# Rewriting the hand-made order of the first quarter in a fused attention and feed-forward kernel

## The chip, the cores and the metric

The kernel runs on one core of one Trainium2 chip. The metric is the device time of one execution in microseconds (us). The engines are named PE (TensorE), DVE (VectorE), ACT (ScalarE), POOL (GpSimd) and SP (SyncE, which here only issues DMAs).

## The reference

Two layers follow each other. The first is attention in which a query sees only the keys of its own cluster: 4 batches, 8 heads, 768 positions, head width 64, 16 clusters per head. The second is a feed-forward layer on the 3072 tokens of width 512, with a softmax-weighted activation of width 1024 and a layer norm.

```python
q_assign = np.argmax(np.einsum('bhsd,hcd->bhsc', q_n, c_n), axis=-1)
k_assign = np.argmax(np.einsum('bhsd,hcd->bhsc', k_n, c_n), axis=-1)
mask = q_assign[:, :, :, None] == k_assign[:, :, None, :]
scores = np.where(mask, scale * np.matmul(q, k.transpose(0, 1, 3, 2)), -1000000000.0)
attn = softmax(scores); attn_out = np.matmul(attn, v)
...
h = x @ w_in
e = np.exp(h - h_max); solu = h * e / (np.sum(e) + 1e-09)
ln = (solu - mu) / np.sqrt(var + 1e-06) * g_ln
return ln @ w_out
```

## The kernel before

The work is cut into 1,814 named steps. Each step has an engine, and each engine works through its steps in one fixed order, which stands as text in the table ORDER (L28 to L72): "xa2 ca E6" is two steps of kind xa, one of kind ca, six of kind E, each time the next of that kind on that engine. A second table, AWAY (L73 to L90), names steps that run on another engine than their default. No step is reordered when the kernel runs: an engine waits at the head of its queue.

One pair of heads (b.p, batch and pair) goes through these steps. SP loads q and k (ld, L375, L433) and v (lv, L551). For batch 0, PE transposes q and k into PSUM (tp, L385) and ACT or DVE evacuates them into a tile xt (xa and xb, L411); for later batches DVE transposes from SBUF instead (xt, L441). A cast (ca, L460) copies a head's 64 rows to bf16 in the tile qk; an index of 1 in the third place means k, which is scaled as it is cast (L472), and 0 means q (L470). PE multiplies xt by the cluster centres (cl, L475). DVE transposes that back (tb), takes the maximum of each group of 16 (mx), compares (oh) and transposes the one-hot rows (ot, L494 to L521). Four placements (pl, L525) copy the one-hot rows beneath q and k in qk, so that one matmul gives scores plus a cluster bias, and bl (L547) zeroes the rows of the odd head. cv (L557) casts v, one step a head.

S is a bank of scores (PE, L618), E its exponential (ACT, L632), V the product with v (PE, L645), and N divides by the row sum (DVE, L658). S22.0 is the first score bank of unit 22. Batch 0 has units 0 to 21: 0 to 3 are pair 0, and the others come two to a group; S4.0 begins pair 1, S8.0 pair 2, S12.0 pair 3, S16.0 turns back to the last columns of all three, and S22.0 begins batch 1. There is one PSUM region for the products V, so the first V of a group waits for the N of the group before it (V2.0 for N0, V4.0 for N1, V8.0 for N3, and so on).

Scores of units 4 to 17 also use two of the three banks of hreg. After that hreg belongs to the feed-forward layer: for a tile f of 128 tokens, tx turns x, h (PE, L742) multiplies by w_in, hm (DVE, L748) takes the maximum, ex (ACT, L753) the exponential, u (DVE, L759) the product, tu turns it, bn and ag (DVE) give the variance, at and al (POOL, L781 and L787) the scale, y (PE, L798) multiplies by w_out, sc scales and ou writes. Once, near the start, w_out is loaded in four parts (lo), summed with its gains on DVE (su0 to su7, L593), averaged by PE (me) and centred by DVE (ce0 to ce7, L606) while the mean stands in a bank of hreg; h1.0.0 needs ce7. w_in is loaded in four parts (li) and cast in eight (wi, POOL). at0 needs ex0.

cp, cb, cq and cf prepare the centres, gt and gk the gains, z and sg are memsets, and fl and wm are matmuls on a blank tile. po is a name in POOL's order with no instruction behind it.

Of the kernel before, what the change touches and what calls it, by code (L numbers as in the profile page):

```python
# [22 lines left out]
class Weave:  # L23
# [19 lines left out]
        fl wm tp2 cp fl4 cl tp2 fl4 cl fl tp S2 cq S tp S tp S2 tp S tp2 S2 cl S V3 S2 tp3 S gt V3
        S2 tp2 S tp S2 cl S3 V3 S7 V3 S3 cl S3 V4 S5 V2 S V2 S4 V S2 V3 S cl S3 V2 S V S2 V S me S3
        V S V3 me S3 ptx V2 S2 cl V S V S5 V2 h4 S2 h V2 S3 h V2 S V2 S h S2 h S V S V2 S V S h S2 h
        V S2 V2 S y3 V S2 y S h2 S2 V2 h2 S2 cl S V S V2 S V S h S2 h S V S V S h y4 S3 V3 h2 S2 V2
        S h S2 V y S y3 S2 V2 S cl S V S V S V2 S2 y S y S2 V3 S2 y S V S y S2 V2 S h S2 V3 S2 cl S
        V3 S3 cl S2 V2 S V2 S h2 S3 h V S V S V2 y3 S2 y V S2 V h S2 V S h S V S h2 S3 h V2 S2 V4 h
        S3 y3 S2 V y S2 V3 S2 h2 S3 V2 cl S3 V2 h S2 h cl V2 S2 V2 S h S2 h2 S2 V3 y S y S y S y V S
        V2 S h2 S2 h2 S3 V3 S V y3 V y V S2 h S cl S3 V2 h S2 h V S2 V S cl V2 S3 y2 S V S V y2 h2  # L50
        S2 V2 S h2 S3 cl S V3 S V S2 y3 S2 V y V S h S2 h V2 S h2 S3 h V2 S y2 S V2 S2 V2 y2 S2 h3
# [5 lines left out]
        cn xb cb tb mx oh ot pl2 tb mx oh ot xa3 cf ca bl cv tb mx oh ot ca2 xa gk su2 N tb mx xa oh
        cv ot su N su2 tb mx N oh su ot N xt2 N su tb mx su oh N xt2 N ce tx ce3 N ce4 hm N ot u N
        bn hm tb N mx oh bn ag ot u xt2 hm cv N bn u bn2 tb mx hm bn N oh ag2 u ot xt2 hm bn N sc u
        bn tb ag cv N xt mx oh xt ot sc N bl xt2 tb bn N mx ca tb N mx oh ot hm oh N ot u xt bn3 ag  # L60
        xt N ag hm sc N ca u bn2 xt bl sc hm ag N xt tb mx u tb oh ot N hm mx xt oh u bn2 ot N hm bn
# [1263 lines left out]
```

## Time and profile before

| what | value |
|---|---|
| median of 3 runs | 223.92 us (223.9 to 224.23) |
| profiled execution, first to last instruction | 222.4 us |
| PE busy | 214.8 us, 97% |
| DVE busy | 199.1 us, 90% |
| ACT busy | 194.7 us, 88% |
| POOL busy | 126.6 us, 57% |
| HBM read and written | 23.11 MB and 6.29 MB |

The profile is of one execution, and its span leaves out what lies before the first and behind the last instruction, so it is 1.5 us under the runs' median. A busy PE is not a PE at its peak, since matmuls are pipelined and their ends are modelled. The same holds for ACT and DVE rows: one instruction's duration overlaps the next one's, so the cost of one in a full queue is the distance between starts. A wait is put down to the semaphore that came last by the profile; where the engine named had long been done, another was the cause.

### The profile page before, as it was taken

To read this page: it belongs to the slowest core of one execution; us is meant where nothing else is said; L and a number is where in the kernel's file an instruction comes from. 1 tells how busy PE (TensorE), PEld (TensorE's weight loads), DVE (VectorE), ACT (ScalarE), POOL (GpSimd) and SP (SyncE) were. 2 spreads that over 40 slices of the span, in tenths; PEclk is the share of its full clock that TensorE was granted. 3 is DMA by queue.
4 is the path that set the end of the run, shared out by engine and by line. 5 is a ranking of instruction groups with operands and counts; after the bars stand their busy time and mean duration, and the time that the engine had idled before them with its cause. 6 is when DMAs were issued, how large, how long until landed. Compare 5 with 4: busy or idle time off the path is not lost.

```text
span 222.4 us, 6852 instructions
## 1 busy us (share of the span) xinstructions
PE 214.8 (97%) x2518; PEld 151.8 (68%) x2548; DVE 199.1 (90%) x363; ACT 194.7 (88%) x382; POOL 126.6 (57%) x252
## 2 busy tenths in 40 slices
...
GB/s 157 352 388 221 193 165 284 203 172 165 127 175 237 180 141 215 136 193 166 153 211 239 156 185 150 151 168 158 230 99 50 115 78 145 117 165 121 166 98 143
DMA packets 122433, 38.74 MB, mean 174 GB/s; under 512 B 111448, under 2 KB 117152, under 8 KB 122400
## 3 DMA queue, kind: packets, MB, share of 16 engines
...
q10 hardware_dynamic: 720, 0.49, 0.7%
...
q14 instruction: 13, 0.11, 0.1%
HBM read 23.11 MB, written 6.29 MB: 132 GB/s over the span
## 4 chain that ended last, share of the span: by engine, by line
PE 91%; DVE 3%; issue 2%; ACT 2%; DVEq 0%; ACTq 0%
PE sps L627 27%; PE hreg L744 18%; PE yps L813 17%; PE ops L654 16%; PE csc L489 4%; PE hreg L627 2%; PE idle_p L859 2%; PE csc L484 1%; PE hreg L403 1%; PE hreg L396 1%; ACT qk L468 1%; PE hreg L813 1%; ACT e L635 1%; DVE u L763 1%; DVE w_sum L598 1%
## 5 line engine op out<-in xcount | busy, mean ns | idle before, releaser
L635 ACT ACTIVATE e<-sps 128x512 bf16<-128x512 f32 (+1 forms) x276 | 143.2, 609 | 10.2 <-PE sps L627 9.8
L627 PE MATMUL sps<-qk 96*128 96x256 bf16 (+5 forms) x600 | 87.4, 263 | 0.7 <-ACT e L635 0.4
L627 PEld LDWEIGHTS <-qk 96*128 96x128 bf16 (+1 forms) x636 | 59.6, 121 | 24.5 <-issue 8.8
L654 PEld LDWEIGHTS <-e 128*128 128x128 bf16 x1152 | 49.9, 97 | 9.3 <-issue 1.9
L654 PE MATMUL ops<-v,e 128*128 128x65 bf16 x1152 | 54.3, 193 | 0.4 <-DVE x L679 0.4
L744 PE MATMUL hreg<-w_in_sb,xT 128*128 128x512 bf16 x177 | 48.3, 378 | 0.8
L813 PE MATMUL yps<-w_out_c,uT 128*128 128x512 bf16 x169 | 45.1, 379 | 0.8
L540 POOL COPY qk<-oht 32x384 f32<-32x384 f32 (+1 forms) x49 | 24.2, 494 | 21.5 <-DVE oht L521 15.7
L763 DVE TENSOR_TENSOR u<-e_sb,hreg 128x1024 bf16<-128x1024 bf16 (+1 forms) x25 | 29.1, 1169 | 2.7 <-ACT e_sb L756 2.1
L774 DVE BATCH_NORM_STATS2 bs<-u 128x6 f32<-128x512 bf16 x48 | 31.3, 677 | 0.0
L750 DVE TENSOR_REDUCE nmax<-hreg 128x1 f32<-128x1024 f32 x24 | 29.1, 1213 | 2.0 <-PE hreg L744 1.7
L756 ACT ACTIVATE e_sb<-hreg,nmax 128x1024 bf16<-128x1024 f32 x24 | 26.9, 1121 | 4.5 <-DVE nmax L750 4.4
L790 POOL TENSOR_SCALAR esq<-es,mv 128x1 f32<-128x1 f32 x24 | 8.3, 344 | 33.6 <-DVE mv L778 30.3
L813 PEld LDWEIGHTS <-uT 128*128 128x128 bf16 x200 | 18.0, 97 | 13.1 <-issue 0.3
L744 PEld LDWEIGHTS <-xT 128*128 128x128 bf16 x192 | 17.6, 97 | 11.3 <-ACT e L635 0.3
L472 POOL TENSOR_SCALAR qk<-xt 64x768 bf16<-64x768 f32 (+1 forms) x27 | 22.2, 823 | 3.5 <-DVE xt L444 1.7
L444 DVE STREAM_TRANSPOSE xt<-raw 128x768 f32<-128x768 f32 x24 | 22.2, 949 | 0.0
L470 POOL CAST qk<-xt 64x768 bf16<-64x768 f32 (+1 forms) x25 | 20.9, 836 | 1.2
L679 DVE TENSOR_TENSOR x<-ops,den 128x256 bf16<-128x256 f32 (+1 forms) x39 | 18.9, 486 | 1.3
L784 POOL TENSOR_SCALAR es<-esum 128x1 f32<-128x1 f32 x24 | 5.6, 236 | 20.9 <-ACT e_sb L756 20.4
L793 POOL TENSOR_TENSOR alpha<-esq,halves 128x1 f32<-128x1 f32 x24 | 13.8, 574 | 2.0
L830 ACT ACTIVATE y<-yps,alpha 128x512 f32<-128x512 f32 x15 | 10.4, 695 | 4.3 <-PE yps L813 3.0
...
## 6 DMA issues: line engine op xcount, KB each, us to landing
...
```

The source lines that it names most:

```text
L444: nc.vector.transpose(xt[:], raws[b, p, i][:].rearrange("p j c -> p (j c)"))
L472: VEC[e].tensor_scalar(dst, src, scalar1=inv_C, scalar2=1.0, op0=Alu.mult, op1=Alu.mult)
L540: ins = VEC[e].tensor_copy(dst.bitcast(F32), src.bitcast(F32).unsqueeze(1) .to_broadcast([NB, 2, n // 2]))
L627: ins = nc.tensor.matmul(sps_[n, k][:, c0:c0 + w], side(b, h // 2, 1, h % 2, keys)[r], side(b, h // 2, 0, h % 2, slice(s0 * P, s0 * P + w) ...
L635: ins = nc.scalar.activation(es[n, k][:, :w], sps_[n, k][:, :w], Act.Exp, scale=exp_scale, bias=-exp_scale)
L654: nc.tensor.matmul(opss[g][:, s, :VW], es[n, k][:, c0:c0 + P], v1[slot(b, h // 2)][:, h % 2, kt, :VW], start=(kt == 0), stop=(kt == n_t - 1))
L744: uses(nc.tensor.matmul(hreg[:, at(f, f2)[1], :], xTs[f][:, dc, :], w_in_sb[:, dc, f2 * FF2:(f2 + 1) * FF2], start=(dc == 0), stop=(dc == ...
L750: uses(nc.vector.tensor_reduce(ff[f, "nmax"][:], pair_of(f), axis=AXY, op=Alu.max, negate=True), *both(f))
L756: uses(nc.scalar.activation(ff[f, "e"][:], pair_of(f), Act.Exp, bias=ff[f, "nmax"][:], accum_out=ff[f, "esum"][:]), *both(f))
L763: uses(nc.vector.tensor_tensor(ff[f, "u"][:, r], ff[f, "e"][:, r], pair_of(f)[:, r], op=Alu.mult), *both(f)[r])
L774: nc.vector.bn_stats(ff[f, "bs"][:, f2, :], ff[f, "u"][:, f2, :])
L813: ins = nc.tensor.matmul(dst, ff[f, "uT"][:, at(f, f2)[0] * (n_fc // 2) + c, :], w_out_c[:, fc, cols], start=(fc == fcs[0] and turn == 0 i ...
```

## The change

The two tables are written anew up to about the first fourth of the run, and nothing else is. The steps, their work and their needs are the same. Each engine's order is new up to these points, and the same behind them: PE up to y0.0, DVE up to u2, ACT up to E3.0, POOL up to at1 (and the name po moves from its end to its start), SP up to the loads of batch 1's third pair.

These steps change engine:

| step | from | to |
|---|---|---|
| xa0.1.0.0, xa0.1.1.0, xa0.3.0.1, xa0.3.1.1 | DVE | ACT |
| xa0.1.1.1, xa0.2.0.0 | ACT | DVE |
| ca0.0.1.0.1 (half a head of k) | ACT | POOL |
| ca0.0.1.1.1 (half a head of k) | POOL | DVE |
| ca0.2.1.0 (k) | ACT | DVE |
| ca0.1.1.0, ca0.1.1.1, ca0.3.1.1 (k) | POOL | DVE |
| ca0.1.0.0, ca0.1.0.1 (q), ca0.2.1.1 (k) | DVE | POOL |
| cv0.0.0, cv0.1.0 | DVE | POOL |
| cv1.1.1 | POOL | DVE |
| pl0.0.1.1.1, pl0.0.1.0.0 (half a pair) | POOL | DVE |

```diff
     ORDER["DVE"] = """
-        cn xb cb tb mx oh ot pl2 tb mx oh ot xa3 cf ca bl cv tb mx oh ot ca2 xa gk su2 N tb mx xa oh
-        cv ot su N su2 tb mx N oh su ot N xt2 N su tb mx su oh N xt2 N ce tx ce3 N ce4 hm N ot u N
...
+        cn xb cb tb mx oh ot pl2 tb mx xa oh ot cf pl xa bl pl ca xa ca tb mx ca oh gk ot su N ca su
+        xt tb mx oh ot su2 N su tb mx oh N ot su xt ca N su tb su N xt mx oh ot N ce2 N ce tx xt N
...
     ORDER["ACT"] = """
-        wa xa2 ca2 xa2 xb ca4 E6 xa E2 xa E xa ca E3 xa3 E4 ca E2 xa E53 ex E13 ex E5 sc E3 ex E11
+        wa xa2 ca2 xa2 xb ca3 xa E2 xa E6 xa E xa ca E3 xa2 E3 xa E2 xa E xa E53 ex E13 ex E5 sc E3
...
     ORDER["SP"] = """
-        ld4 si ld3 lv lg ld3 lo lv lo ld2 lo2 lv ld6 lv ld8 li4 tx ld3 lv ld tx lv tu ld10 tx tu ld4
+        ld4 si ld3 lv lg ld3 lo lv ld4 lo2 ld lv li ld3 lo ld4 lv ld li ld3 li2 tx ld lv tx ld4 lv
...
```

Three places show the new order best. The line numbers of the new kernel are two higher. The first is DVE from the end of pair 3's cluster search (mx, oh, oht are its maximum, one-hot rows and turned rows) to N3; den and x are the two instructions of an N, w_sum is an su, xt<-raw is a transpose of batch 1, and qk_102<-xt is a cast for pair 3. Before:

```order
L510 TENSOR_REDUCE mx<-cst 128x24
L666 RECIPROCAL den<-ops 128x4
L679 TENSOR_TENSOR x<-ops,den 128x2x2x64
L515 TENSOR_TENSOR oh<-cst,mx 128x384
L598 SCALAR_TENSOR_TENSOR w_sum<-w_g,g_ln_115,w_sum 128x512
L521 STREAM_TRANSPOSE oht<-oh 128x384
L666 RECIPROCAL den<-ops 128x4
L679 TENSOR_TENSOR x<-ops,den 128x2x2x64
L444 STREAM_TRANSPOSE xt<-raw 128x768 x2
```

After:

```order
L512 TENSOR_REDUCE mx<-cst 128x24
L517 TENSOR_TENSOR oh<-cst,mx 128x384
L668 RECIPROCAL den<-ops 128x4
L681 TENSOR_TENSOR x<-ops,den 128x2x2x64
L523 STREAM_TRANSPOSE oht<-oh 128x384
L600 SCALAR_TENSOR_TENSOR w_sum<-w_g,g_ln_115,w_sum 128x512
L446 STREAM_TRANSPOSE xt<-raw 128x768
L474 TENSOR_SCALAR qk_102<-xt 64x6x128
L668 RECIPROCAL den<-ops 128x4
L681 TENSOR_TENSOR x<-ops,den 128x2x2x64
```

The last den and x of both pieces are N3. One transpose of batch 1 and a k cast of pair 3 now stand in front of it; the other transpose of batch 1 stands further ahead, in front of pair 2's tb.

The second place is POOL from the blank of pair 1 to that of pair 2. qk_100, qk_101 and qk_102 are the tiles of pairs 1, 2 and 3; qk<-oht is a placement, qk<-xt a cast, v a cast of v. Before:

```order
L549 MEMSET qk_100 16x384
L470 CAST qk_102<-xt 64x6x128
L533 COPY qk_100<-oht 32x6x64
L470 CAST qk_102<-xt 64x6x128
L533 COPY qk_101<-oht 32x6x64
L558 CAST v_1_106<-vf 128x6x64
L1290 MEMSET v_1_106 128x12x2
L1290 MEMSET v_2_107 128x12x2
L533 COPY qk_101<-oht 32x6x64 x3
L472 TENSOR_SCALAR qk_102<-xt 64x6x128
L549 MEMSET qk_101 16x384
```

After:

```order
L551 MEMSET qk_100 16x384
L535 COPY qk_100<-oht 32x6x64 x2
L560 CAST v_1_106<-vf 128x6x64
L472 CAST qk_102<-xt 64x6x128 x2
L535 COPY qk_101<-oht 32x6x64 x2
L560 CAST v_1_106<-vf 128x6x64
L551 MEMSET qk_101 16x384
L535 COPY qk_101<-oht 32x6x64
L560 CAST v_2_107<-vf 128x6x64
L535 COPY qk_101<-oht 32x6x64
```

Pair 2's blank moved ahead of its last two placements, and two casts of v now stand between the placements.

The third place is POOL around at0 (es<-esum). qk_103 is the tile of batch 1's first pair, v_4 its v. Before:

```order
L578 CAST w_in_sb<-w_st 128x512 x7
L470 CAST qk_103<-xt 64x768
L472 TENSOR_SCALAR qk_103<-xt 64x768 x2
L784 TENSOR_SCALAR es_1229<-esum 128x1
L540 COPY qk_103<-oht 32x2x192 x4
L1290 MEMSET v_4_109 128x12x2
L558 CAST v_4_109<-vf 128x6x64
```

After:

```order
L580 CAST w_in_sb<-w_st 128x512 x3
L542 COPY qk_103<-oht 32x2x192 x2
L580 CAST w_in_sb<-w_st 128x512
L542 COPY qk_103<-oht 32x2x192
L580 CAST w_in_sb<-w_st 128x512 x3
L786 TENSOR_SCALAR es_1229<-esum 128x1
L560 CAST v_4_109<-vf 128x6x64 x2
L474 TENSOR_SCALAR qk_103<-xt 64x768
L542 COPY qk_103<-oht 32x2x192
```

Three of the four placements moved ahead of at0, between the casts of w_in; two casts of v and a k cast now stand between at0 and the fourth.

More of the change, by code (lines that the diff above doesn't have):

```diff
@@ L39 @@
-        pl2 al pl2 ca2 bl ca at al ca pl2 cv2 pl ca3 al ca3 pl at2 pl3 al2 ca2 pl ca at cv pl cv at
-        ca at cv al pl2 bl pl al at3 al2 at al2 at al at al2 at2 po at al3
+        po pl2 ca bl z ca pl2 ca2 cv ca cv pl2 ca bl pl2 cv ca2 pl2 cv bl pl cv pl ca pl cv sg pl z
+        pl z bl pl ca cv z wi cv ca wi3 pl2 wi pl wi3 at cv2 ca pl ca3 bl al pl2 ca3 at pl2 z bl ca3
+        al at al pl4 at ca cv ca cv ca cv al bl ca3 pl4 ca2 pl4 at2 pl2 bl ca cv pl al2 ca2 cv2 ca2
+        at cv ca4 al pl4 at2 cv bl cv3 pl2 al pl2 ca2 bl ca at al ca pl2 cv2 pl ca3 al ca3 pl at2
@@ L41 @@
+        pl3 al2 ca2 pl ca at cv pl cv at ca at cv al pl2 bl pl al at3 al2 at al2 at al at al2 at3
+        al3
     """
     ORDER["PE"] = """
[L43 to L51, printed above, removed]
@@ new lines @@
+        me S2 V3 me S2 V S4 V2 S V2 S3 V ptx S V S V2 S2 cl S V S2 h V h3 S V S h V S3 h V2 S V2 S h
+        S2 h S V S V S V2 S h S2 h V S2 V S V y3 V S2 y S h2 S2 V2 h2 S2 cl S V S V2 S V S h S2 h S
+        V S V S h y4 S3 V3 h2 S2 V2 S h S2 V y S y3 S2 V2 S cl S V S V S V2 S2 y S y S2 V3 S2 y S V
+        S y S2 V2 S h S2 V3 S2 cl S V3 S3 cl S2 V2 S V2 S h2 S3 h V S V S V2 y3 S2 y V S2 V h S2 V S
+        h S V S h2 S3 h V2 S2 V4 h S3 y3 S2 V y S2 V3 S2 h2 S3 V2 cl S3 V2 h S2 h cl V2 S2 V2 S h S2
@@ new lines @@
+        h2 S2 V3 y S y S y S y V S V2 S h2 S2 h2 S3 V3 S V y3 V y V S2 h S cl S3 V2 h S2 h V S2 V S
+        cl V2 S3 y2 S V S V y2 h2 S2 V2 S h2 S3 cl S V3 S V S2 y3 S2 V y V S h S2 h V2 S h2 S3 h V2
+        S y2 S V2 S2 V2 y2 S2 h3 S3 V2 h2 V y S3 y3 V3 S3 h2 S2 cl S V S V S V2 S y2 h V S2 h V S2
+        h2 S2 V S V h V4 S2 y2 h S3 V2 h2 S2 V2 S y2 S2 h2 y2 S h2 S2 V2 y S V2 S y h2 S3 h2 S2 V4 y
+        S3 h2 y V S2 h2 V S V S V y4 S2 V h4 S3 y V3 y S2 y2 h4 y S V3 y V y2 h ptx h y h2 y3 h2 y4
@@ L55 @@
+        h2 ptu2 y8 ptu y4 ptu y4
     """
     ORDER["DVE"] = """
[L57 to L61 removed]
```

53 lines of the change are left out of this document (26 added, 27 removed).

## The prediction

> **What bounds the kernel now.** I read the page's span first, then the busy time by stage, then the timeline of each engine at the places where the order changes.
>
> ```profile
> span 222.4 us, 6852 instructions
> 8.00:24.10 16.10, 15.19 (x179) 9.86 (x172) 14.62 (x32) 15.67 (x39) 11.77 (x20) 1.00 0.97 323
> 24.10:34.00 9.90, 9.69 (x148) 7.36 (x149) 9.52 (x19) 9.78 (x22) 8.13 (x15) 1.00 0.87 151
> 34.00:47.10 13.10, 13.05 (x172) 9.31 (x170) 12.56 (x24) 12.93 (x27) 10.14 (x18) 1.00 0.90 242
> 60.00:220.00 160.00, 157.50 (x1754) 109.87 (x1779) 147.50 (x256) 140.33 (x267) 85.30 (x165) 1.00 0.80 157
> ```
>
> Each stage row gives the stretch, its length, the busy time of PE, weight load, DVE, ACT and POOL, the granted clock, and DMA. From 60 us on PE is busy 157.5 of 160 us, with an order that the change leaves alone: a head start there is carried to the end. Before that three engines are full at once. So I ask where PE stands idle in the rewritten stretch, and which engine is late there next. The clock is 1.00 throughout, so no term comes from it.
>
> PE's timeline where the first batch's second head pair begins (start, duration, and idle time in brackets):
>
> ```profile
> 21.42 0.66 PE L627 MATMUL sps<-qk 96*128 96x384 bf16 x3
> 22.46 0.74 PE L654 MATMUL ops<-v,e 128*128 128x65 bf16 x18 [0.38 <-DVE x L679]
> 23.04 0.65 PE L627 MATMUL sps<-qk 96*128 96x384 bf16 x3
> 24.09 0.60 PE L627 MATMUL hreg<-qk 80*128 80x256 bf16 x4 [0.40 <-DVE xt L430]
> 29.58 0.82 PE L627 MATMUL sps<-qk 80*128 80x256 bf16 x6
> 30.24 0.54 PE L654 MATMUL ops<-v,e 128*128 128x65 bf16 x12
> 31.44 1.22 PE L627 MATMUL sps<-qk 96*128 96x256 bf16 x6
> ```
>
> The pace is in the rows from 29.58: six score matmuls of 256 columns go out in 30.24 - 29.58 = 0.66 us, 0.11 each, so three of 384 columns need 0.49. (In the last row six took 1.22: there PE waited for ACT to free score slots.) The first group was out at 21.91 and V2.0 began at 22.46; the second at 23.53 and S4.0 began at 24.09. PE lost 0.55 + 0.56 = 1.1 us, both to DVE: to N0, and to the evacuation xa0.3.1.1 that sat in DVE's queue behind mx0.2. Both go: the new order has N0 right behind su0, and that evacuation on ACT.
>
> **Part 1, ACT.** Four evacuations come to ACT; two evacuations, half a k cast and a full k cast leave.
>
> ```profile
> 8.68 2.02 ACT L468 ACTIVATE qk<-xt 64x384 bf16<-64x384 f32 x4
> 10.61 2.34 ACT L635 ACTIVATE e<-sps 128x384 bf16<-128x384 f32 x6
> 17.19 1.27 ACT L430 COPY xt<-hreg 128x384 f32<-128x384 f32 x3
> 19.83 0.86 ACT L468 ACTIVATE qk<-xt 64x768 bf16<-64x768 f32 x1
> 20.56 0.88 ACT L635 ACTIVATE e<-sps 128x384 bf16<-128x384 f32 x2
> ```
>
> From start to start a half cast takes (10.61 - 8.68) / 4 = 0.48, a full cast 20.56 - 19.83 = 0.73; an evacuation takes 1.27 / 3 = 0.42. ACT loses 0.48 + 0.73 - 2 x 0.42 = 0.4 us net. With that and PE's 1.1 us, S4.0 can come about 1.0 us earlier, at 23.1. What is late next is POOL, whose placements S4.0 needs:
>
> ```profile
> 17.68 2.16 POOL L533 COPY qk<-oht 32x384 f32<-32x384 f32 x3
> 25.23 0.93 POOL L533 COPY qk<-oht 32x384 f32<-32x384 f32 x1 [2.28 <-DMA raw<-in_q_dram]
> 26.92 2.18 POOL L533 COPY qk<-oht 32x384 f32<-32x384 f32 x3
> 30.05 0.41 POOL L549 MEMSET qk<- 16x384 f32 x1
> 45.71 1.72 POOL L472 TENSOR_SCALAR qk<-xt 64x768 bf16<-64x768 f32 x2
> 52.46 0.51 POOL L558 CAST v<-vf 128x384 bf16<-128x384 f32 x1
> L533 POOL COPY qk<-oht x12: 497/614/934, 17.7 to 34.5; 32x384 f32<-32x384 f32 x12
> ```
>
> The first row is pl0.1, and the last gives minimum, median and maximum of a placement in ns. pl0.1 began at 17.68. Now a k cast stands ahead of it on DVE (0.54 to 0.81, below), so it begins at 18.3; four copies, a cast, a blank and 0.4 of gaps (4 x 0.61 + 0.86 + 0.41 + 0.4 = 4.1) end at 22.4, and at 23.7 with all copies at 0.93. I take the median: S4.0 keeps 23.1.
>
> **Part 2, POOL before S8.0.** Before, POOL stood idle 2.28 us until DVE's turned one-hot rows were there (the DMA that the row names had landed), and pl0.2 ended at 26.92 + 2.18 = 29.10, just ahead of S8.0 at 29.58. In the new order a v cast and two q casts follow pl0.1 (22.4 + 0.51 + 2 x 0.86 + 0.2 = 24.8), then come four copies, two v casts and a blank: 4 x 0.61 + 2 x 0.51 + 0.41 and 0.4 of gaps, to 29.1. The head start at S8.0 is then about 0.4, not 1.0; with all copies at 0.93 it would be -0.9. ACT works a few scores behind PE, so I keep its 1.0 us, and let PE catch up where it waited for slots in the row at 31.44.
>
> **Part 3, DVE up to N3.** V8.0 needs N3, the normalisation of the group before it, since there is one output bank group. Four k casts of a full head, half a cast, two placements and two evacuations come to DVE; four evacuations, two q casts, a k cast and two v casts leave; both transposes of batch 1 now stand in front of N3.
>
> ```profile
> 8.99 0.57 DVE L540 COPY qk<-oht 32x192 f32<-32x192 f32 x2
> 11.10 1.45 DVE L430 COPY xt<-hreg 128x384 f32<-128x384 f32 x3
> 14.10 0.36 DVE L558 CAST v<-vf 128x384 bf16<-128x384 f32 x1
> 15.17 0.58 DVE L497 STREAM_TRANSPOSE cst<-csc 128x384 f32<-128x384 f32 x1 [0.71 <-PE csc L484]
> 32.05 1.83 DVE L444 STREAM_TRANSPOSE xt<-raw 128x768 f32<-128x768 f32 x2
> 34.45 0.78 PE csc L489 x8
> L472 DVE TENSOR_SCALAR qk<-xt x3: 541/543/810, 18.1 to 163.9; 64x768 bf16<-64x768 f32 x3
> L470 DVE CAST qk<-xt x4: 541/556/691, 13.1 to 126.8; 64x768 bf16<-64x768 f32 x4
> ```
>
> Coming: 0.57 + 2 x 0.48 + 0.35 + 4 x 0.54 + 1.83 = 5.87. The 0.48 is 1.45 / 3, and the 0.35 an estimate: half of 0.54 to half of 0.81. Leaving: 4 x 0.48 + 0.69 + 0.56 + 0.81 + 2 x 0.36 = 4.70, and the 0.71 of idle time. N3 made way for the transposes at 32.05, so now at 32.05 + 5.87 - 4.70 - 0.71 = 32.5. PE reaches V8.0 from S8.0 at 29.2 by nine score banks of two matmuls, four value products ((23.04 - 22.46) / 3 = 0.19 each) and cl1.0, which is 9 x 0.22 + 4 x 0.19 + 0.78 = 3.5, at 32.7. No wait by this sum; if each k cast takes the 0.81 that one took at 18.1, N3 ends at 33.6 and PE waits 0.9 us.
>
> That 0.81 is the price while POOL was copying: the three copies from 17.68 on took 0.72 each, where the fastest take 0.50. Both engines were slow together. The Trainium skill, Perfetto Trace Analysis, section Optimizing Scalar/DVE Operations, states that GPSIMD and DVE share an SBUF read port, so that moving operations between those two might not help. By that rule the sum would be the 33.6. The two later k casts of 0.54 show that it does not hold each time here.
>
> **Part 4, DVE to the first feed-forward tile.** h1.0.0 needs ce7, ex0 needs hm0.
>
> ```profile
> 34.27 0.18 DVE L666 RECIPROCAL den<-ops 128x4 f32<-128x4 f32 x1 [0.40 <-PE ops L654]
> 44.40 2.71 DVE L607 SCALAR_TENSOR_TENSOR w_out_c<-w_g,g_ln,hreg 128x512 bf16<-128x512 f32 x4
> 47.13 1.23 DVE L750 TENSOR_REDUCE nmax<-hreg 128x1 f32<-128x1024 f32 x1
> 48.86 0.57 DVE L521 STREAM_TRANSPOSE oht<-oh 128x384 bf16<-128x384 bf16 x1
> 48.39 1.11 ACT L756 ACTIVATE e_sb<-hreg,nmax 128x1024 bf16<-128x1024 f32 x1
> ```
>
> From N3 to the end of ce7 (44.40 + 2.71) it was 47.11 - 32.05 = 15.06. The two transposes (1.83) and an idle 0.40 go, ot1.0 (0.57) comes: 13.4. So ce7 ends at 45.9 and hm0 at 47.2 instead of 48.36, 1.2 us earlier; with N3 at 33.6 it is 0.1 earlier. ex0 followed hm0 at once (48.36 to 48.39), so these are the two ends of its head start; ACT's own 1.0 caps the upper. I take 0.65, near the middle, since the copies' median 614 ns against 497 at best says that part of them meet DVE.
>
> **Part 5, POOL before S22.0.** The new order puts two v casts and a k cast between at0 and the last placement of batch 1's first pair; before, four placements followed at0.
>
> ```profile
> 49.75 0.24 POOL L784 TENSOR_SCALAR es<-esum 128x1 f32<-128x1 f32 x1 [2.32 <-ACT e_sb L756]
> 50.05 2.16 POOL L540 COPY qk<-oht 32x384 f32<-32x384 f32 x4
> 52.26 0.38 PE L627 MATMUL sps<-qk 80*128 80x256 bf16 x2
> ```
>
> at0 waits for ex0. From its end at 49.99 the old four took to 52.21, and S22.0 began at 52.26. The new four need 2 x 0.51 + 0.86 + 0.50 and about 0.1 of gaps, 2.48 in place of 2.22. So S22.0 loses 0.25 of the head start: 0.65 - 0.25 = 0.4 us. Nothing behind it in the changed tables waits sooner than before.
>
> The SP order is rewritten too: batch 1's first load goes ahead of the last three quarters of w_out, and DVE turns it well before the 32.05 of the row above. DMA is busy 0.97 in the first stage row, so that load could be late. I take 0, since it also stands further ahead in SP's queue; a late one would cost about what the idle 0.40 at 34.27 did.
>
> **The sum.** The profiled execution's span is 222.4; the runs' median is 223.92, so 1.5 us lie outside the span and stay. 222.4 - 0.4 + 1.5 = 223.5 us. A measurement of this kernel can tell 0.2% (0.45 us) from no change: this forecast lies on that edge.
>
> **Rivals.** *The whole head start comes through:* k casts at 0.54, POOL's copies at 0.50, v casts ready, so ex0 leads by the capped 1.0 and S22.0's placement hides behind PE's own work: 222.9. For it: DVE's later casts; against: the S22.0 sum. *DVE and POOL slow each other (the slower side):* all k casts at 0.81 put N3 at 33.6 and V8.0 waits 0.9 us; hm0 leads 0.1 at best, and lags 0.25 if the placements on POOL and the two sums of su beside them slow down as much; S22.0 takes 0.25 more. It decides from a lead of 0.25 and below at ex0, where nothing is left after S22.0: +0.5, 224.4. For it: 0.81 and 0.72 at 17.7 to 18.9; against: 0.54 later. The page of the Trainium skill named above states the rule behind it. *It changes nothing:* DVE's work cancels its idle time and PE stands where it stood at 52.26: 223.9.
>
> **Chances.** Forecast 0.40 (half of it beyond the edge: 0.19 faster, 0.20 same, 0.01 slower); whole head start 0.22, all faster; slower rival 0.22 (0.18 slower, 0.04 same); nothing 0.16 (0.13 same, 0.02 slower, 0.01 faster). Faster 0.42, same 0.37, slower 0.21. The range 222.8 to 224.5 takes in both outer cases; the forecast's own is 223.2 to 223.8.
>
> **What would show it.** Right: S4.0 near 23.1 and no idle time in front of V2.0 and S4.0; hm0 ending near 47.7; POOL's last placement before S22.0 as PE's releaser. Wrong: PE waiting for N3 at V8.0, DVE k casts at 0.8, hm0 ending after 48.4, xt1.0.0 waiting for its load, or a PE wait at a place that I have not named.

## The result and the profile after

The new order is slower by 0.7%: 225.51 us in the median of four runs (225.4 to 225.77) against 223.95 for the kernel before, a ratio of 1.0071 (95% interval 1.0056 to 1.0086). The forecast was 223.5 us, its range ended at 224.5.

The first view of the changed kernel is its span, then the first two stage rows as shown of before (stretch, length, busy time of PE, weight load, DVE, ACT, POOL, granted clock, DMA), then the waits of PE from 17 to 54 us (total, times, longest).

```profile
span 223.2 us, 6880 instructions
```
```profile
8.00:24.10 16.10, 15.80 (x178) 10.41 (x176) 15.45 (x34) 15.73 (x40) 11.85 (x21) 1.00 0.98 305
24.10:34.00 9.90, 8.40 (x123) 5.62 (x120) 9.51 (x17) 8.83 (x19) 9.14 (x15) 1.00 0.89 215
```
```profile
PE sps L629 <- POOL qk L535: 1.8, 2, 1.5
PE sps L629 <- ACT e L637: 0.2, 1, 0.2
```

In the first stretch PE is busier than before (15.80 against 15.19): the two waits for DVE are gone. In the second it has lost more than it won (8.40 against 9.69 of 9.90 us), ACT with it (8.83 against 9.78), while POOL's busy time rose from 8.13 to 9.14. The clock is 1.00 as before. The waits name the engine, POOL, and the line of the placements. PE's timeline (start, duration, idle time in brackets) shows where:

```profile
22.23 0.96 PE L629 MATMUL sps<-qk 96*128 96x384 bf16 x3
23.03 0.60 PE L629 MATMUL hreg<-qk 80*128 80x256 bf16 x4
...
28.56 0.38 PE L629 MATMUL hreg<-qk 96*128 96x256 bf16 x2
30.44 0.81 PE L629 MATMUL sps<-qk 80*128 80x256 bf16 x6 [1.50 <-POOL qk L535]
...
36.01 0.38 PE L629 MATMUL sps<-qk 80*128 80x256 bf16 x2 [0.34 <-POOL qk L535]
```

The row at 23.03 is S4.0, without a wait, where it stood at 24.09. The row at 30.44 is S8.0, at 29.58 before; the one at 36.01 is S12.0, at 35.40 before. Both now wait for the last placement of their pair. POOL's timeline of the same stretch:

```profile
18.53 1.16 POOL L535 COPY qk<-oht 32x384 f32<-32x384 f32 x2 [1.75 <-DVE oht L523]
19.78 1.67 POOL L474 TENSOR_SCALAR qk<-xt 64x768 bf16<-64x768 f32 x1
21.49 0.41 POOL L551 MEMSET qk<- 16x384 f32 x1
21.94 1.04 POOL L535 COPY qk<-oht 32x384 f32<-32x384 f32 x2
23.04 0.71 POOL L560 CAST v<-vf 128x384 bf16<-128x384 f32 x1
23.70 2.05 POOL L472 CAST qk<-xt 64x768 bf16<-64x768 f32 x2
25.81 1.41 POOL L535 COPY qk<-oht 32x384 f32<-32x384 f32 x2
27.29 0.84 POOL L560 CAST v<-vf 128x384 bf16<-128x384 f32 x1
28.19 0.41 POOL L551 MEMSET qk<- 16x384 f32 x1
28.55 0.50 POOL L535 COPY qk<-oht 32x384 f32<-32x384 f32 x1
29.11 0.71 POOL L560 CAST v<-vf 128x384 bf16<-128x384 f32 x1
29.89 0.50 POOL L535 COPY qk<-oht 32x384 f32<-32x384 f32 x1
30.47 1.34 POOL L474 TENSOR_SCALAR qk<-xt 64x768 bf16<-64x768 f32 x1
...
33.92 0.12 POOL L1292 MEMSET v<- 128x24 bf16 x1
...
35.47 0.50 POOL L535 COPY qk<-oht 32x384 f32<-32x384 f32 x1
```

From pair 1's first placement at 18.53 to pair 3's last, which ends at 35.97, POOL has no idle time of more than 0.1 us; before, it stood idle 2.28 us in this stretch. The placements are mostly at 0.50 us. What is long are casts: 1.67 for a k cast (0.83 in other rows), 2.05 for two q casts, 0.71 to 0.84 for v casts (0.50 at best).

The two profiled executions did not start alike. The first cluster product cl0.0.0 began at 6.32 us in this execution and at 6.71 in the profiled one of before, with the same instructions ahead of it; in the profiles of this study it began between 5.89 and 6.77. The times as they stand so flatter the changed kernel by 0.39 us, and stages are compared below by the time since cl0.0.0. Counted so, S4.0 came at 16.71 instead of 17.38, S8.0 at 24.12 instead of 22.88, and S12.0 at 29.69 instead of 28.69. From there on PE hardly waits, and the 1.0 us stays to the end. Another 0.21 us is lost between S44.0 and S46.0, where no wait is shown. About 0.3 us more lies outside the span: the changed kernel's spans (223.2 to 223.5) are 2.2 to 2.3 under its times, while 17 other executions of before had spans around 221.9 (221.2 to 222.4), 2.0 under theirs. The three make up the 1.56 us of the medians within 0.1.

### The profile page after: what moved, and what is told of

The parts are those of the page before. It is cut to its first block, busy times and chain, and to the rows that moved or that the text cites. A ratio compares the mean times of both kernels' runs of the same rounds, so it can differ in the third digit from the quotient of the medians.

```text
span 223.2 us, 6880 instructions
## 1 busy us (share of the span) xinstructions
PE 216.3 (97%) x2548; PEld 151.2 (68%) x2548; DVE 200.3 (90%) x364; ACT 194.7 (87%) x382; POOL 127.2 (57%) x251
## 4 chain that ended last, share of the span: by engine, by line
PE 89%; ACT 5%; POOL 3%; issue 1%; DVE 1%; DVEq 0%; ACTq 0%; POOLq 0%
PE sps L629 26%; PE hreg L746 18%; PE yps L815 18%; PE ops L656 15%; PE csc L491 4%; ACT e L637 3%; PE idle_p L861 2%; PE hreg L629 1%; PE csc L486 1%; POOL qk L535 1%; ACT xt L432 1%; PE hreg L815 1%; PE hreg L398 1%; POOL qk L474 1%; ACT qk L470 0%
## 5 line engine op out<-in xcount | busy, mean ns | idle before, releaser
L629 PE MATMUL sps<-qk 96*128 96x256 bf16 (+5 forms) x600 | 88.4, 263 | 2.2 <-POOL qk L535 1.8
L656 PEld LDWEIGHTS <-e 128*128 128x128 bf16 x1152 | 51.0, 97 | 10.1 <-issue 2.0
L656 PE MATMUL ops<-v,e 128*128 128x65 bf16 x1152 | 55.6, 193 | 0.1
L746 PE MATMUL hreg<-w_in_sb,xT 128*128 128x512 bf16 x192 | 51.4, 379 | 0.0
L815 PE MATMUL yps<-w_out_c,uT 128*128 128x512 bf16 x184 | 47.4, 378 | 0.0
L542 POOL COPY qk<-oht 32x384 f32<-32x384 f32 (+1 forms) x47 | 23.5, 500 | 19.9 <-DVE oht L523 14.4
L765 DVE TENSOR_TENSOR u<-e_sb,hreg 128x1024 bf16<-128x1024 bf16 (+1 forms) x25 | 29.1, 1169 | 3.5 <-ACT e_sb L758 3.0
L752 DVE TENSOR_REDUCE nmax<-hreg 128x1 f32<-128x1024 f32 x24 | 29.1, 1213 | 1.9 <-PE hreg L746 1.5
L472 POOL CAST qk<-xt 64x768 bf16<-64x768 f32 (+1 forms) x27 | 22.8, 843 | 2.2 <-DVE xt L432 0.8
L560 POOL CAST v<-vf 128x384 bf16<-128x384 f32 x26 | 14.5, 567 | 0.8
```

The costliest lines, as they stand in the source:

```text
L472: VEC[e].tensor_copy(dst, src)
L542: ins = VEC[e].tensor_copy(dst.bitcast(F32), src.bitcast(F32).unsqueeze(1) .to_broadcast([NB, 2, n // 2]))
L629: ins = nc.tensor.matmul(sps_[n, k][:, c0:c0 + w], side(b, h // 2, 1, h % 2, keys)[r], side(b, h // 2, 0, h % 2, slice(s0 * P, s0 * P + w) ...
L656: nc.tensor.matmul(opss[g][:, s, :VW], es[n, k][:, c0:c0 + P], v1[slot(b, h // 2)][:, h % 2, kt, :VW], start=(kt == 0), stop=(kt == n_t - 1))
L746: uses(nc.tensor.matmul(hreg[:, at(f, f2)[1], :], xTs[f][:, dc, :], w_in_sb[:, dc, f2 * FF2:(f2 + 1) * FF2], start=(dc == 0), stop=(dc == ...
L752: uses(nc.vector.tensor_reduce(ff[f, "nmax"][:], pair_of(f), axis=AXY, op=Alu.max, negate=True), *both(f))
```

## The experiments

**Theories.** A: POOL's queue is late, and sets S8.0 and S12.0. Rival B: DVE, which got more work, is what is late. Rival C: the new order of the loads. All times in this table are counted from the start of cl0.0.0, in one profiled execution of each kernel, the column "end" is the end of the span, and the last two columns are the runs' medians of the kernel and of the kernel before on the same chip.

| kernel | pair 2's last placement ends | S8.0 | pair 3's last placement ends | S12.0 | V12.0 | S22.0 | end | us | before |
|---|---|---|---|---|---|---|---|---|---|
| before | 22.39 | 22.88 | 28.34 | 28.69 | 32.16 | 45.55 | 215.67 | | |
| after | 24.07 | 24.12 | 29.64 | 29.69 | 33.70 | 46.52 | 216.85 | 225.51 | 223.95 |
| e1 q casts behind | 22.21 | 22.45 | 30.25 | 30.30 | 34.31 | 47.12 | 217.46 | 225.54 | 223.92 |
| e2 k cast on DVE | 23.58 | 23.64 | 29.90 | 29.95 | 33.96 | 46.78 | 217.10 | 225.87 | 223.92 |
| e4 no sums | 22.55 | 22.61 | 27.96 | 28.01 | 32.02 | 44.97 | 215.67 | 224.72 | 223.92 |
| f1 memsets early | 24.84 | 24.89 | 30.21 | 30.26 | 34.27 | 47.08 | 217.41 | 225.49 | 223.76 |
| f2 both | 22.48 | 22.54 | 29.62 | 29.67 | 33.68 | 46.49 | 216.82 | 224.99 | 223.76 |
| f3 and DVE's k cast | 22.76 | 22.81 | 29.90 | 29.95 | 33.96 | 46.77 | 217.11 | 225.25 | 223.76 |
| g1 early start | 22.89 | 22.94 | 29.21 | 29.27 | 33.28 | 46.09 | 216.44 | 225.27 | 223.89 |
| g2 POOL sorted | 22.30 | 22.36 | 28.27 | 28.55 | 33.52 | 46.34 | 216.66 | 225.50 | 223.89 |
| g3 DVE sorted | 22.26 | 22.32 | 28.22 | 28.50 | 33.37 | 46.19 | 216.53 | 224.55 | 223.44 |
| g4 N5 forward | 22.25 | 22.31 | 28.22 | 28.50 | 32.52 | 46.09 | 216.43 | 225.17 | 223.71 |
| b1 DVE's two places | 21.88 | 22.07 | 27.78 | 27.93 | 31.40 | 44.79 | 214.91 | 223.36 | 223.76 |
| b2 k cast off ACT | 22.34 | 22.39 | 28.63 | 28.68 | 31.85 | 45.15 | 215.50 | 223.78 | 223.91 |
| b3 POOL's load | 21.62 | 22.10 | 27.56 | 27.96 | 31.43 | 44.82 | 214.94 | 223.29 | 223.91 |

How to read it: in eight rows (after, e1, e2, e4, f1, f2, f3, b2) S12.0 starts 0.05 us behind pair 3's last placement, in g1 0.06. There POOL released it. In before, g2 to g4, b1 and b3 the distance is 0.15 to 0.40, and PE came there by itself.

The last columns need care. What lies outside the span (time minus span, the median over a kernel's executions) is 2.0 us for before, on which b1 to b5 stand, and 1.9 to 2.0 for these; it is 1.8 for e1, f2, f3 and g3, and 2.0 to 2.5 for after and the other kernels with the new tables. So half a microsecond between two times need not come from the stages at all, and the experiments are read by the stages. By the column "end" the change costs 1.18 us, and among the edits of the changed kernel that leave all the work in, none gives more than 0.42 of it back.

**e1: the q casts of pair 3 behind pair 2's placements.**

```diff
 ORDER["POOL"], after
-... ca bl pl2 cv ca2 pl2 cv bl pl cv pl ca pl ...
+... ca bl pl2 cv pl2 cv bl pl cv pl ca3 pl ...
```

> The changed kernel with two casts of q for pair 3 (ca0.3.0.0 and ca0.3.0.1) moved on POOL from ahead of the four placements of pair 2 to behind them; nothing else. Theory A (POOL is the late engine, and has no idle time from pair 1's placements to the last of pair 3): the last placement of pair 2 ends about 2.0 us earlier than the 30.39 of the changed kernel, so the wait in front of S8.0 goes, but POOL has as much to do before S12.0 as it had, so S12.0 stays at 36.0 within 0.4, and the time at 225.5 within 0.3. If only the order in front of S8.0 was the cost: S12.0 near 35.2 and the time 224.6. Rival B (DVE is late): V8.0 waits for N3 at 33.6, and the time stays at 225.5, with N3 as PE's releaser. Rival C (the loads in SP's new order): no change.

225.54 us in the median (225.14 to 228.63), the same; by the stages it is 0.6 later. S8.0 came 1.7 us earlier (22.45), as theory A has it, and S12.0 did not (30.30, later by 0.6). PE's waits in this kernel name one that I had not thought of:

```profile
PE ops L656 <- POOL v L1292: 1.4, 1, 1.4
PE sps L629 <- ACT e L637: 0.5, 1, 0.5
```

L1292 is z2, the memset of 0.12 us beside pair 2's v, which V8.0 reads. The new order has it among pair 3's placements (the row at 33.92 above), the old one had it at 26.73. The order in front of S8.0 alone was not the cost; POOL's queue up to S12.0 was as long as ever.

**e2: the 1.67 us k cast from POOL to DVE.**

```diff
+AWAY ca0.2.1.1: DVE
 ORDER["POOL"]
-... pl2 ca bl pl2 cv ca2 ...
+... pl2 bl pl2 cv ca2 ...
 ORDER["DVE"]
-... su N ca su xt tb ...
+... su N ca2 su xt tb ...
```

> The changed kernel with one k cast (ca0.2.1.1) moved from POOL, where it took 1.67 us, to DVE, behind the other k cast of that pair. Theory A (POOL late): the last placement of pair 2 ends at 28.7 to 29.2 in place of 30.39 and that of pair 3 at 34.5 to 35.0 in place of 35.96; S8.0 and S12.0 come 1.0 to 1.4 earlier, and the time is 224.3 (224.0 to 224.8). Rival B (DVE late): DVE gets 0.55 to 0.75 us more to do ahead of pair 2's one-hot rows and of N3, so that N3 ends at 34.2 and the time is 225.6 to 226.2. Rival C (loads): 225.5.

225.87 us: theory A's 224.3 was wrong, rival B's 225.6 to 226.2 came out. The waits are shared now:

```profile
PE sps L629 <- POOL qk L535: 1.1, 2, 0.6
PE ops L656 <- DVE x L681: 0.7, 2, 0.6
```

Pair 2's turned one-hot rows came 19.06 us after cl0.0.0 instead of 17.68: the cast cost DVE 0.76, the sum behind it took 0.89 and the comparison oh0.2 1.02 where the fastest take 0.71 and 0.55. POOL then stood idle for 1.1 us, waiting for DVE. So neither engine has room for this cast.

**e3: the old order of the loads in the changed kernel.** SP's text of before, nothing else.

> The changed kernel with the order of the loads on SP as it was before; all other engines as in the changed kernel. Rival C (the new order of the loads costs the time): 224.0 to 224.5, and S8.0 and S12.0 earlier. Theory A and rival B: S8.0 and S12.0 stand within 0.3 us of 30.4 and 36.0, and the time is 225.5 within 0.3, unless batch 1's first load, which is now later in the queue, makes DVE's transpose at 20.7 wait, which would make it longer, by up to 1 us.

231.93 us, 3.7% over before. DVE's row of the transpose that the new order has brought forward:

```profile
25.81 0.98 DVE L446 STREAM_TRANSPOSE xt<-raw 128x768 f32<-128x768 f32 x1 [4.91 <-POOL qk L472]
```

DVE stood 4.9 us in front of it, until the load landed (25.63; the engine named in the brackets had long been done), and all of DVE's queue with it. The granted clock also fell, to 0.91 from 20 to 60 us, so the size means little. The new loads belong to the new DVE order, and undoing them is no cure.

**e4: five sums over w_out left out.** su1 to su5 are skipped when the steps are issued.

> The changed kernel with five of the eight sums over w_out (su1 to su5 on DVE) left out, so the mean that is taken from w_out is not the whole one. Theory A with a collision (these sums read two tiles of SBUF, and POOL's casts beside them are slow): POOL's casts of q and k go back to 0.82 to 0.9 us where they took 1.17 and 1.34, ca0.2.1.1 from 1.67 to about 1.1; the last placement of pair 2 ends at 29.2 or earlier in place of 30.39, that of pair 3 at 34.5 or earlier in place of 35.96; the time is 224.4 or less. If POOL's slow casts have nothing to do with the sums: they stay at 1.1 to 1.7 and POOL stays late, 225.2 to 225.5. Rival B (DVE late): DVE has 4.4 us less to do and N3 comes early, the time falls by over 1 us, while POOL's casts stay slow.

224.72 us, 0.8 less. POOL's rows in this kernel:

```profile
19.83 1.01 POOL L474 TENSOR_SCALAR qk<-xt 64x768 bf16<-64x768 f32 x1
...
23.27 1.70 POOL L472 CAST qk<-xt 64x768 bf16<-64x768 f32 x2
...
29.01 0.82 POOL L474 TENSOR_SCALAR qk<-xt 64x768 bf16<-64x768 f32 x1
```

They answer to 1.67, 2.05 and 1.34 above, and are 1.5 us shorter together. The sums on DVE were what made POOL's casts slow, as the collision had it. Leaving them out also takes work off DVE, but POOL began pair 1's placements 12.2 us after cl0.0.0 in both kernels and waited for nobody from there on, so the 1.7 us by which S12.0 comes earlier (28.01) is what POOL's own instructions took less. The time shows only half of it: the 12 executions of this kernel range from 224.17 to 226.64, and the profiled one (224.24) is among the shortest.

**f1, f2, f3: POOL's queue mended step by step.** f1 takes z2, z3 and sg to POOL's idle time in front of pair 1's placements; f2 is f1 with e1's edit; f3 is f2 with DVE's k cast ca0.1.1.1 behind ot0.1.

```diff
 ORDER["POOL"], f2 and f3 (f1 without the move of ca2)
-... ca cv pl2 ca bl pl2 cv ca2 pl2 cv bl pl cv pl ca pl cv sg pl z pl z bl pl ca ...
+... ca cv z2 sg pl2 ca bl pl2 cv pl2 cv bl pl cv pl ca3 pl cv pl2 bl pl ca ...
 ORDER["DVE"], f3
-... tb mx ca oh gk ot su N ca ...
+... tb mx oh gk ot ca su N ca ...
```

> The changed kernel with three memsets (z2, z3 and sg) moved on POOL from among pair 3's placements to its idle time in front of pair 1's placements (16.78 to 18.53). z2 writes the ones beside pair 2's v, which V8.0 reads; it ended at 34.04 and V8.0 began at 34.09. Theory A (POOL's full queue sets S8.0 and S12.0, and z2 in it also V8.0): S8.0 stays at 30.4, V8.0 comes 0.2 to 0.4 earlier (N3, at 33.58, or PE's own pace is next), pair 3's last placement ends 0.45 earlier, at 35.5, S12.0 at 35.6 and the time is 225.1 (224.9 to 225.3). If POOL's end is not what S12.0 waits for: 225.5.

> The changed kernel with both edits: the three memsets early, and the two casts of q for pair 3 behind pair 2's placements. Theory A: S8.0 near 28.7 counted from the changed kernel's start, V8.0 no longer behind z2 but behind N3 (about 33.2), pair 3's last placement 0.45 earlier than with the q casts alone, and so is S12.0; the time is 225.0 (224.7 to 225.2). If the wait in front of S8.0 and V8.0 set the time and not POOL's total: 224.2.

> As the kernel with both edits, and DVE's k cast ca0.1.1.1 moved from ahead of pair 1's one-hot rows to behind their turning (ot0.1), so that POOL can begin pair 1's placements about 0.6 us earlier. Theory A: POOL's whole queue moves 0.4 to 0.6 us forward, pair 3's last placement and S12.0 with it, and the time is 224.5 (224.2 to 224.8). Rival B (DVE is as late as POOL): pair 2's and 3's one-hot rows come no earlier, POOL gets idle time instead, and the time is 224.9 to 225.1.

f1: 225.49, no gain, 225.1 expected. Its profiled execution shows another chance wait, 1.1 us of PE for pair 2's load of k (below). f2: 224.99, the expected number, but by luck as far as the changed kernel goes. V8.0 came at 27.26 instead of e1's 28.17, so z2 was what e1 had waited for, and S12.0 came 0.6 earlier than in e1; it stands at 29.67, where the changed kernel has it, and the 0.5 us against that kernel lies outside the span (1.8 for 2.3). f3: 225.25, where 224.5 was expected. POOL's row in front of pair 2:

```profile
24.90 1.78 POOL L535 COPY qk<-oht 32x384 f32<-32x384 f32 x2 [1.80 <-DVE oht L523]
```

POOL began pair 1's placements 0.8 us earlier than in f2, then stood idle 1.8 us instead of 0.4, as rival B has it, and pair 3's last placement ended at 29.90: pair 2's one-hot rows came 0.28 later from DVE (18.23 for 17.95), and from pair 2's last placement on POOL took 7.14 us in both. A head start of POOL is not kept while DVE's queue is as full.

**f4: the k cast to ACT,** on top of f2.

> The changed kernel with the memsets early, the two casts of q for pair 3 behind pair 2's placements, and the k cast ca0.2.1.1 moved from POOL to ACT, ahead of pair 1's last exponentials. Theory A: POOL's queue is 0.8 to 1.7 us shorter, pair 3's last placement ends at 34.3 to 34.9 counted from the changed kernel's start instead of 35.9, ACT is 0.73 us later up to there, and the time is 224.3 (224.0 to 224.7). If POOL's load is not what S12.0 waits for, or ACT is as full: 225.0 to 225.4.

228.54 us in the median, with executions of 225.25 to 229.95, some at a granted clock of 0.99; the profiled one waited 1.6 us in front of pair 2's turn of k, whose load landed at 14.24 instead of 12.88. It settles nothing.

**b1: the kernel before, with DVE's two places put right.** Here the question is turned round: what would the two waits that the change removed have been worth by themselves?

```diff
 ORDER["DVE"], before
-... xa gk su2 N tb mx xa oh cv ot ...
+... xa gk su N su xa tb mx oh cv ot ...
```

> The kernel before with only the two places on DVE put right at which PE waited 0.55 and 0.56 us: N0 ahead of the sum su1, and the evacuation xa0.3.1.1 ahead of pair 2's cluster search; POOL, ACT, SP and PE in the old order, and no step on another engine. Theory A: S4.0 comes 0.4 to 1.0 us earlier, but S8.0 needs pair 2's last placement, which ended at 29.10 against S8.0 at 29.58, and S12.0 pair 3's, at 35.05 against 35.40, so at most 0.4 us is kept: 223.6 (223.4 to 223.9). If PE's two waits were all that counts: 222.9. If ACT is full: 223.9.

223.36 against 223.76, a ratio of 0.9984 (0.9973 to 0.9995): S4.0 came at 16.48, as early as with the whole change (16.71). The time moved by the 0.4 us that theory A named as the most, but not for its reason: it took the placements of pairs 2 and 3 to stay where they were, and they came 0.5 to 0.6 earlier; in the profile S12.0 leads by 0.76 and the end by as much.

**b2 and b3: POOL's load in the old order.** b2 moves ca0.2.1.0 from ACT to POOL; b3 instead gives POOL two steps that the change gives it, ca0.2.1.1 and cv0.1.0, from DVE. Both on top of b1.

```diff
 ORDER["POOL"], b2
-... ca pl3 bl ca pl ca pl cv ...
+... ca pl3 bl pl ca3 pl cv ...
 ORDER["POOL"], b3
-... ca pl3 bl ca pl ca pl cv ...
+... ca pl2 ca pl bl ca pl cv ca pl cv ...
```

> The kernel before with the two places on DVE put right, and one k cast (ca0.2.1.0) moved from ACT to POOL, behind pair 1's last placement, where POOL had 1.7 us of idle time in front of pair 2's placements. In the run with the two places alone ACT had no idle time from 14 to 31 us, and POOL did not hold PE up. Theory A, continued (with POOL early enough, ACT's queue of exponentials is next): ACT's exponentials of pair 1 come up to 0.7 us earlier, POOL's idle time takes the cast up, and the time is 223.0 (222.6 to 223.3). If PE's own pace is next: 223.4. If POOL's cast meets DVE's sums and pair 2's placements come late: 223.6 to 224.0.

> The kernel before with the two places on DVE put right, and two of the steps that the change gives to POOL given to it there: the k cast ca0.2.1.1 between pair 1's placements and the v cast cv0.1.0 behind them, both from DVE. Theory A: POOL gets 1.5 to 2.4 us more in front of pair 2's placements, of which its idle 1.7 us takes up most; pair 2's and pair 3's last placements end 0 to 0.9 us later than without, S8.0 and S12.0 then wait for them, and the time is 223.9 (223.4 to 224.3). Rival B (DVE is what is late): DVE has 1.2 us less to do, and the time is 222.6 to 223.2.

b2: 223.78, no gain; S4.0 stood still, so ACT was not what came next there, and pair 3's placements came 0.85 us later than in b1. b3: 223.29, a ratio of 0.9969 (0.9957 to 0.9982), where theory A expected 223.9. POOL's load alone is not the cost: in the old order the cast ca0.2.1.1 took 0.83 us, and POOL's idle time took both steps up, since DVE was the lighter by them and gave its one-hot rows earlier (17.69 against 17.95 in b1).

**b4, twice, and b5: the new order of the loads in the old kernel.** b5 has w_in's four loads where they were. The second run of b4 was made to see one of its longer executions.

```diff
 ORDER["SP"], before
-... lo lv lo ld2 lo2 lv ld6 lv ld8 li4 tx ...
+... lo lv ld4 lo2 ld lv li ld3 lo ld4 lv ld li ld3 li2 tx ...
```

That is b4, and this is b5:

```diff
 ORDER["SP"], before
-... lo lv lo ld2 lo2 lv ld6 lv ld8 li4 tx ...
+... lo lv ld4 lo2 ld lv ld3 lo ld4 lv ld4 li4 tx ...
```

> The kernel before with the new order of the loads on SP alone. Rival C (the loads cost something): over 224.1, with waits for w_out or for w_in. Theory A: 223.8 within 0.3, since nothing that engines wait for in the old order comes later than it is used.

> The kernel before with the new order of the loads alone, a second time, for a profile of one of its longer executions (spans were 222.0 to 223.8). Rival C: a span over 222.8 shows an engine waiting for a load of w_out, w_in or of pair 2's k, by 0.5 to 1.5 us. If no wait shows and the span is long: the cause is not a load that engines wait for.

> The kernel before with the new order of the loads on SP, but the four loads of w_in where they were. Rival C, by the loads of w_in (now among batch 1's, so that w_in's last part or batch 1's k comes late in some executions): 223.8 within 0.3. Rival C, by batch 1's first load ahead of w_out's: 224.5 to 225.2, as with the whole new order.

b4: 224.86 and 225.00, ratios 1.0043 (1.0025 to 1.0060) and 1.0045 (1.0030 to 1.0060). b5: 224.15, 1.0015 (0.9997 to 1.0033). In the second profile of b4, PE and DVE:

```profile
PE xtp L719 <- DVE x L679: 0.7, 1, 0.7
```
```profile
40.16 0.98 DVE L444 STREAM_TRANSPOSE xt<-raw 128x768 f32<-128x768 f32 x1 [0.94 <-ACT e L635]
```

That is the transpose xt1.1.1 of batch 1's second k; its load now stands behind two of w_in, and landed at 39.98. N6 and PE's first turn of x stand behind it. Rival C is right for the old kernel: 0.4% for the whole new order of the loads, and with w_in's loads where they were no difference can be told. In the changed kernel this transpose stands 4 us later, and from S12.0 to S18.0 nothing is lost (8.65 us, before 8.68). The changed kernel was not run with w_in's loads alone put back.

**g1 to g4: start and content, then DVE.** g1 lets POOL start early (on DVE it has f3's edit, on PE and ACT the turn of pair 2's k and its evacuation go behind pair 1's cluster product and scores); g2 adds the memsets and puts cv0.2.0 behind pair 2's last placement; g3 moves tb1.0 on DVE and ca1.0.0.0 on POOL; g4 moves xt1.1.0 on DVE.

```diff
 g1: ORDER["PE"]
-... tp S2 tp S cl V3 S3 gt ...
+... tp S3 cl V3 S3 tp gt ...
 g1: ORDER["ACT"]
-... E2 xa E xa ca E3 xa2 E3 ...
+... E2 xa E ca E3 xa3 E3 ...
 g2: ORDER["POOL"]
-... ca cv pl2 ca bl pl2 cv ca2 pl2 cv bl pl cv pl ca pl cv sg pl z pl z bl pl ca ...
+... ca cv z2 sg pl2 ca bl pl2 cv ca2 pl2 cv bl pl2 cv ca pl cv pl2 bl pl ca ...
 g3: ORDER["DVE"]
-... N su tb su N xt mx oh ot N ce2 ...
+... N su2 N tb xt mx oh ot N ce2 ...
 g3: ORDER["POOL"]
-... bl pl ca cv z wi cv ...
+... bl pl cv z wi ca cv ...
 g4: ORDER["DVE"]
-... N su2 N tb xt mx oh ot N ce2 ...
+... N su2 N tb mx oh ot N xt ce2 ...
```

> The changed kernel with pair 1's one-hot rows forward: the k cast ca0.1.1.1 on DVE behind their turning (ot0.1), and PE's turn of pair 2's k (tp0.2.1.0, with its evacuation xa0.2.1.0 on ACT) behind pair 1's cluster product and scores, where the old order had it. Theory A with the late start as its cause: POOL begins pair 1's placements 0.8 to 1.2 us earlier, all behind it in its queue moves with it, S12.0 comes 0.8 to 1.2 us earlier and the time is 224.5 (224.2 to 224.8). If the cause is what stands in the queue: POOL's head start is used up by waits for pair 2's and 3's one-hot rows or by slower casts, S12.0 moves by 0.3 at most, and the time is 225.2 to 225.5.

> As the kernel with the early start, with the three memsets in POOL's early idle time and the v cast cv0.2.0 behind pair 2's last placement. Theory A (the queue's content counts as well): S8.0 comes another 0.5 to 0.7 us earlier, S12.0 another 0.3 to 0.5, and the time is 224.1 (223.8 to 224.4). If the start alone counts: as the kernel with the early start, within 0.2.

> The changed kernel with POOL's queue sorted and started early, and in addition DVE's first turn for batch 1 (tb1.0) behind su7 and N4, and POOL's first cast for batch 1 (ca1.0.0.0), which ran beside su6 and su7 there, behind the first cast of w_in. If DVE is the next engine that is late (theories A and B both hold, one behind the other): su7 ends 0.8 to 1.2 us earlier, the mean (me0) no longer waits, and the time is 224.7 (224.3 to 225.0). If DVE's end before the first feed-forward tile (ce7) sets the time whatever stands ahead of su7: 225.3 to 225.6.

> The changed kernel with POOL's queue sorted and started early, tb1.0 behind N4, and in addition the transpose xt1.1.0 on DVE behind N5. If DVE's order was what was left: N5 ends about 0.8 us earlier, V12.0 waits 0.1 us at most, and the time is 223.8 (223.5 to 224.1). If DVE has too much to do up to ce7, wherever it stands: the wait moves to ce7, and the time is 224.4 to 224.7.

g1: 225.27, S12.0 0.4 earlier; the early start is worth less than half of what was expected. g2: POOL's last placement of pair 3 ends at 28.27, as early as before the change, and S12.0 comes at 28.55. The time is 225.50, not 224.1. PE's waits and the later of them in its timeline say why:

```profile
PE ops L656 <- DVE x L681: 0.7, 1, 0.7
PE hreg L606 <- DVE w_sum L600: 0.6, 1, 0.6
```
```profile
36.50 0.70 PE L606 MATMUL hreg<-w_sum,g_mean 128*128 128x256 f32 x2 [0.60 <-DVE w_sum L600]
```

The 0.7 stands early, 23.9 us after cl0.0.0: with S8.0 on time PE waits for N2 in front of V6.0. The 0.6 is the mean's wait for DVE's last sum, right behind S12.0, and takes most of the 1.1 us won there back: S13.0 is 0.27 earlier than in the changed kernel, S22.0 0.18. g3: 224.55, near the expected 224.7, but S22.0 came only 0.15 earlier than in g2; the rest lies outside the span (1.8 for 2.3) and in the kernel before on that chip (223.44). The wait for the sum is gone, and V12.0 now waits for N5 instead, 0.14 us behind its end. (The row names a cast for batch 1 that V12.0 does not need.) g4: V12.0 comes 0.85 earlier (32.52), and the wait moves to V14.0, which begins 0.06 behind N6. The rows of g3 and g4, in this order:

```profile
39.84 0.54 PE L656 MATMUL ops<-v,e 128*128 128x65 bf16 x12 [0.79 <-POOL qk L472]
```
```profile
41.87 0.36 PE L656 MATMUL ops<-v,e 128*128 128x65 bf16 x6 [0.61 <-DVE x L681]
```

S22.0 is only 0.1 earlier than in g3, and the time is 225.17. DVE's waits from 30 to 48 us are 0.1 us each at most in this kernel, and ce7 ends 40.9 us after cl0.0.0, before 40.4. Neither expected branch came out in its numbers (223.8, or the wait at ce7 and 224.4 to 224.7); what the second one says of the cause fits, for DVE's queue is full and each step moved forward makes PE wait for a later one.

**What follows.** Theory A holds for the changed kernel as it is: POOL's last placements release S8.0 and S12.0, which g2's 28.55 shows as well, and e4 shows that DVE's sums are what makes POOL's casts long. Rival B holds behind it: once POOL is put right, DVE takes back 0.7 to 1.0 us of the 1.1 to 1.2 won at S12.0 (g2 to g4). Both engines have no room in the new order, and each slows the other. Rival C is not the cause here. Not settled: the 0.2 us between S44.0 and S46.0, which the kernels with the new tables have, all but f4, and none with the old (b2 loses as much two units later); and why the time outside the span differs between kernels (1.7 to 2.5 us).

## Why the prediction was wrong

**Bounds and S4.0: right in kind, two thirds of the size.** V2.0 and S4.0 no longer wait. S4.0 came at 23.03, forecast 23.1, but that is in part luck: 0.39 us of it is this execution's earlier start, and since cl0.0.0 the gain is 0.67 for the forecast 1.0. ACT's lead is alike: its last exponential ahead of S8.0 began 22.84 us after cl0.0.0, before 23.43, that is 0.6 for 1.0.

**Part 2, POOL before S8.0: the step that failed.** It took pair 2's last placement to end at 29.1, "a head start of about 0.4". In the time of the old profile, that is by the distance from cl0.0.0, it ended at 30.78, and S8.0 came 1.24 us later than before. The sum, term by term:

| term | forecast | measured |
|---|---|---|
| pl0.1 begins, in the time of the old profile | 18.3 | 18.92 (18.53 as it stands) |
| four placements, k cast, blank, gaps | 4.1 | 4.45 (the cast 1.67 for 0.86) |
| v cast, two q casts, gaps | 2.4 | 2.77 (0.71 + 2.05 for 0.51 + 1.72) |
| four placements, two v casts, blank, gaps | 4.3 | 4.64 (v casts 0.84 and 0.71 for 0.51) |

The start is the largest miss. The one cast counted ahead of it took 0.59, as priced, but pair 1's cluster search on DVE also began later (9.12 us after cl0.0.0 for 8.46), with no idle time in front of it, and that was put at nothing. The list of steps was right and the median price of the placements too high; the casts were priced as if DVE stood still. The other end that the text gave, -0.9 at S8.0 with all placements slow, was nearer to what came (-1.24), for another reason than the one it named, and it was kept out of the range. The same queue then goes on to pair 3: the prediction stopped reading POOL at S8.0, named no wait at S12.0, and let ACT and PE "catch up". e1 shows that S12.0 waits even if S8.0 does not.

**Part 3, DVE up to N3.** The forecast had N3 0.45 us later, and 1.5 later if each k cast took 0.81. It ended 27.26 us after cl0.0.0, before 25.41: 1.85 later. By the distance between starts the four k casts took 2.45 for 2.16, the half cast 0.58 for 0.35, and two placements that came to DVE 1.24 for 0.57; the longer of these is the row

```profile
12.98 0.83 DVE L542 COPY qk<-oht 32x192 f32<-32x192 f32 x1
```

Evacuations, two fewer on balance, saved 0.70 for 0.96. The sums are not in it: two of them are long,

```profile
23.92 2.38 DVE L600 SCALAR_TENSOR_TENSOR w_sum<-w_g,g_ln,w_sum 128x512 f32<-128x512 f32 x2
```

1.14 and 1.20, but one was as long before (1.18), and the six up to N3 took 4.7 us for 4.9. V8.0 came 3.65 us behind S8.0, 3.5 by the forecast's count of PE's work, so it did not wait for N3, since S8.0 was late already. That DVE is late too came out only in f3 and in g2 to g4.

**Parts 4 and 5, the loads.** hm0 ended at 48.94, forecast near 47.7; since cl0.0.0 that is 0.97 later than before, so it followed PE's loss. S22.0 lost nothing to the steps behind at0: from S12.0 it was 16.83 us, before 16.86, and the last placement ended 0.09 ahead of PE. The 0 for the loads was right in this kernel. One wait was missed: PE turns pair 2's k 2.7 us earlier than in the old order, close behind its load (landed 12.88, turned at 13.01), and in f1's execution it waited 1.1 us there.

**The span.** The prediction added 1.5 us to a span of 222.4. That execution was 0.5 longer than most, and 2.0 lies outside; the two cancel in the sum, and no step follows from it, but the forecast's starting point was a long run set equal to a median.

**The rivals.** The slower one had the right mechanism, DVE and POOL slowing each other, at the wrong place (N3 and V8.0 for S8.0 and S12.0) and so at a third of the price: +0.5 for +1.6.
